# Attention followed by a gated FFN: how eighteen weight steps are spread, and how each finds its scale

## The chip, the cores and the metric

The kernel runs on one core of a Trainium2 chip. A core has five engines, each with an instruction queue of its own that it works off in order: TensorE (PE, matmuls; PEld is its weight load), VectorE (DVE), ScalarE (ACT), GpSimd (POOL) and SyncE (SP, which here only issues transfers). Sixteen DMA engines carry the transfers of all queues. The metric is the time of one execution in device microseconds (us).

## What is computed

```python
# attention: batch 8, heads 8, seq 576, head_dim 64, all float32
scores = q @ k.T / 8 + min(-(cum_i - cum_j), 0)   # cum: running sum of max(s, 0); causal mask
attn   = softmax(scores)
x      = (attn @ v), heads side by side           # 4608 tokens x 512
# gated FFN, weights float64: w_gate, w_val 512 x 1536; w_out 1536 x 512
out = (sigmoid(x @ w_gate) * (x @ w_val)) @ w_out # float32
```

## The kernel before

Attention goes head by head: 64 heads, numbered i, two of a pair sharing q, k and v tiles. A head has five query tiles of up to 128 rows. The main loop runs over *ticks* n; a tick is one query tile, so five ticks make one head. The first eight heads (batch 0, ticks 0 to 39) are computed with float32 matmuls; the later ones with q, k, probabilities and v split into float16 high and low parts, whose tiles are turned round by transposing transfers ("T<-qk", "pt<-p").

The result of a head pair is transposed on PE into a PSUM tile `nx_ps` and split into float16 parts x (L686, L688 on ACT, L689 on DVE). That PSUM tile has the tag "av" with one buffer.

The FFN works in units: a group of 256 tokens and one of 12 slices of 128 columns (`ffn_in`). A unit is 24 matmuls into a PSUM tile "gv" of two buffers (L714), a tanh on ACT (L719) and a product on DVE, `t2f` (L721). Groups 0 and 1 need only batch 0; their 24 units start at tick NE = 44 and fill PE's room beside the attention of the next heads. The second half of a unit (`ffn_out`, L744) needs all weights.

The weights arrive as float64 and are read as pairs of 32-bit integers. Eighteen *weight steps*, numbered n, turn them into float16 high and low parts: steps 0 to 11 one column slice of w_gate and w_val each (o = 0), steps 12 to 17 two row slices of w_out each (o = 1). A step is:

- two transfers of 512 KB (`load_weight`). Buffers rotate by three for steps 0 to 11: step n can be loaded and decoded when step n-3 has given back its buffers. Each `weight_step` also issues the loads that have become possible.
- `decode_weight`: a copy on ACT (L298) and three integer operations on DVE (L299, L300, L301) that rebuild a float32 in `a`. L299 leaves the magnitude's bits in `m`, which is the place where the result will go.
- a scale, a power of two. `split_weight` has two ways to find it. With `m`: `column_bound` sums the upper halves of `m` over the rows by eight matmuls with a matrix of ones into a PSUM tile `wps` (L310), takes the largest on DVE (L313), and two operations on one element a row make the scale (L332, L334). Without `m` (a path that the kernel has, and that float64 weights did not take): a Square on ACT with its sum along each row, a sum over the rows on POOL (`partition_all_reduce`), and `pow2_of`, two DVE operations.
- the high part, a copy with the scale on ACT (L337), and the low part on DVE (L338).

`column_bound` takes its PSUM tile from tag "av" (one buffer) up to tick 39 and from tag "o" (two buffers, shared with the outputs of attention and FFN) after it.

Steps 0 and 1 stand at tick 0 in the program, steps 2 to 5 at ticks 8, 16, 24 and 32; steps 6 to 17 are written between ticks 46 and 48, where the FFN's units call for them. The program order is not the order on the chip: a planner sorts the instructions of each engine by priority (program order, unless `first()` raises it) and by times that it works out itself, so that an instruction whose inputs and buffers are ready can come long before its place. `first()` is put around the float32 attention and, from tick 44 to 86, around the scores and outputs of the later heads.

Of the kernel before, what the change touches and what calls it, by code (L numbers as in the profile page):

```python
# [10 lines left out]
F32 = mybir.dt.float32  # L11
F32R = mybir.dt.float32r
I32 = mybir.dt.int32
I64 = mybir.dt.int64
AF = mybir.ActivationFunctionType
ALU = mybir.AluOpType
ADD_REDUCE = bass.bass_isa.ReduceOp.add

P = 128
# [6 lines left out]
def tile_attention_then_gated_ffn(  # L26
# [11 lines left out]
    nc = tc.nc  # L38
# [11 lines left out]
    NTL = len(TILES)  # L50
# [4 lines left out]
    NN = H  # L55
# [7 lines left out]
    pp = ctx.enter_context(tc.tile_pool(name="pp", bufs=2, space=bass.MemoryType.PSUM))  # L63
# [69 lines left out]
    wscale = cp.tile([P, 2, NF], F32, name="wscale")  # L133
# [8 lines left out]
    def first(now=True):  # L142
        return tc.high_priority(1000) if now else ExitStack()
# [80 lines left out]

    wide = w_gate.dtype == I64
    wst, wdec, wtot = {}, {}, {}

    rows_out = cp.tile([P, 2 * DM], F32, name="io")
    t2big = cp.tile([P, 2 * NF * GT], F32, name="t2f")
# [60 lines left out]
    def decode_weight(n):  # L290

        o, f = wsteps[n]
        r, a, _ = room(n)
        if not wide:
            return a.bitcast(F32), None
        m = w2all[:, f // 2].rearrange("p l h x n -> p (l h x n)") if o else w1[f].rearrange("p c g l n -> p (c g l n)")
        m = m.bitcast(I32)
        nc.scalar.activation(a.bitcast(F32), r[:, :, 1].bitcast(F32), AF.Copy, scale=2.0 ** -112)  # L298
        nc.vector.tensor_scalar(m, a, 3, 0x7FFFFFF8, ALU.logical_shift_left, ALU.bitwise_and)  # L299
        nc.vector.scalar_tensor_tensor(a, a, -0x80000000, m, ALU.bitwise_and, ALU.bitwise_or)  # L300
        nc.vector.scalar_tensor_tensor(a, r[:, :, 0], 29, a, ALU.logical_shift_right, ALU.bitwise_or)  # L301
        return a.bitcast(F32), m

    def column_bound(n, m):

        top = m.bitcast(BF16).rearrange("p (n t) -> p n t", t=2)[:, :, 1]
        early = wnext["tick"] < NTL * NN
        ps = pp.tile([P, 512], F32, tag="av" if early else "o", name=f"wps{n}", **({"bufs": 1} if early else {}))
        for c in range(8):
            nc.tensor.matmul(ps[:, :P], ones, top[:, c * P : (c + 1) * P], start=c == 0, stop=c == 7)  # L310
        tot = wp.tile([P, 1], F32, tag="wst", name=f"wtot{n}")
        junk = lp.tile([P, P], BF16, tag="wj", name=f"wj{n}")
        nc.vector.tensor_scalar(junk, ps[:, :P], 2.0 ** -100, None, ALU.max, ALU.max, accum_out=tot)  # L313
        return tot

    def split_weight(n, a, m):

        o, f = wsteps[n]
        if o:
            hi, lo = (w2all[:, f // 2, l].rearrange("p h x n -> p (h x n)") for l in range(2))  # L320
        else:
            a = a.rearrange("p (c n) -> p c n", n=P)
            hi, lo = (w1[f].rearrange("p c g l n -> p (c g) l n")[:, :, l] for l in range(2))
        if m is None:
            ss = wp.tile([P, 1], F32, tag="wss", name=f"wss{n}")
            nc.scalar.activation(hi, a, AF.Square, accum_out=ss)
            tot = wp.tile([P, 1], F32, tag="wst", name=f"wtot{n}")
            nc.gpsimd.partition_all_reduce(tot, ss, P, ADD_REDUCE)
            pow2_of(wscale[:, o, f : f + 1 + o], tot, f"w{n}")
        else:  # L330
            e = wp.tile([P, 1], I32, tag="xe", name=f"xe_w{n}")
            nc.vector.tensor_scalar(e, column_bound(n, m).bitcast(I32), 0x7F800000, None, ALU.bitwise_and)  # L332
            dst = wscale[:, o, f : f + 1 + o]
            nc.vector.tensor_scalar(dst.bitcast(I32), e.to_broadcast([P, 2]) if o else e, -1.0, 268.0 * 2.0 ** 23,  # L334
                                    ALU.mult, ALU.add)
        sc = wscale[:, o, f : f + 1]
        nc.scalar.activation(hi, a, AF.Copy, scale=sc)  # L337
        nc.vector.scalar_tensor_tensor(lo, a, sc, hi, ALU.mult, ALU.subtract)  # L338
# [21 lines left out]
        osc[b] = wp.tile([P, 1], F32, tag="osc", name=f"osc{b}", bufs=3)  # L360
        nc.vector.tensor_scalar(osc[b], gmax, sv[b][1], 2.0 ** 14, ALU.mult, ALU.mult)

    wnext = {"load": 0, "step": 0, "tick": 0}

    def weight_step():
        n = wnext["step"]
# [425 lines left out]
    NE, NOFF = 44, 87  # L792
# [6 lines left out]
    for n in range(nticks + 12):  # L799
        if n == NTL * EARLY:  # L800
            more_room()
        i, t = divmod(n, NTL)
        wnext["tick"] = n
        if i < NN:
            with first():
                n_s(i, NTL - 1 - t)
# [37 lines left out]
        if i < NH:  # L844
            p, j = divmod(i, 2)
            b, h = divmod(i, H)
            if t == 0 and i + 1 < NH:
                load_crow(i + 1)
            if t == (2 if i >= NN else 0) and i + 1 < NH:
                spread_crow(i + 1)  # L850
            if i + 2 < NN:
                if j == 0 and t == 1:
                    n_load(p + 1)
                    load_v(p + 1)
                if j == 1 and t == 2:
                    with first():
                        n_prep(p + 1)
            elif j == 0 and i + 2 < NH:
                if t == (2 if spare else 1 if i >= NN else 0) and p + 1 not in qk32:
                    load_qk(p + 1)  # L860
                if t == 2 and i < NN:
                    load_v(p + 1)
            if NN <= i and i + 1 < NH and j == 1 and t == 2:
                load_v(p + 1)
            if NN <= i and j == 0 and t == 0:
                split_v(p)
            if not spare:
                late = i >= NN
                if i + 2 >= NN and j == 0:
                    if t == 2 + late:  # L870
                        qk_square(p + 1)
                    if t == 3 + late:
                        qk_scale(p + 1)
                if n == NTL * (NN - 1) - 1 or NN <= i and t == 0:
                    split_qk(max(i + 1, NN))
                if n == NTL * (NN - 1) + 1 or NN <= i and t == 2:
                    swap_k(i + 1)
            elif i <= EARLY + 1:
                if j == 0:
                    if t == 1:  # L880
                        split_qk(i + 1)
                    if t == 3:
                        swap_k(i + 1)
                        load_qk(p + 2)
                else:
                    if t == 0:
                        qk_square(p + 1)
                    if t == 1:
                        qk_scale(p + 1)
                    if t == 2:  # L890
                        split_qk(i + 1)
                    if t == 4:
                        swap_k(i + 1)
                        split_qk(i + 2)
                        load_qk(p + 3)
            elif j == 0 and i + 2 < NH:
                if t == 0:
                    if i == EARLY + 2:
                        swap_k(i + 1)
                    qk_square(p + 1)  # L900
                if t == 1:
                    qk_scale(p + 1)
                if t == 2:
                    split_qk(i + 2)
                if t == 4:
                    swap_k(i + 2)
            elif j == 1 and i + 2 < NH:
                if t == 1:
                    split_qk(i + 2)
                if t == 3:  # L910
                    swap_k(i + 2)
                    if i + 6 < NH:
                        load_qk(p + 3)
            if b == 0:
                if 1 <= n < 1 + vch:
                    v_square(0, n - 1)
                if n == 1 + vch:
                    v_scale(0)
            if b == 0:
                if t == 2 and 1 <= h < 1 + vch:  # L920
                    v_square(1, h - 1)
                if t == 4 and 1 <= h < 1 + vch:
                    v_square_sum(1, h - 1)
                if t == 1 and h == 6:
                    v_scale(1)
            elif b == 1:
                if VSQ <= n < VSQ + vch:
                    v_square(2, n - VSQ)
                if VSQ + 5 <= n < VSQ + 5 + vch:
                    c = VSQ + 4 + vch - n  # L930
                    v_square_sum(2, c)
                if n == VSQ + 11:
                    v_scale(2)
            elif b + 1 < B:
                if t == 0 and 2 <= h < 2 + vch:
                    v_square(b + 1, h - 2)
                if t == 4 and 2 <= h < 2 + vch:
                    v_square_sum(b + 1, h - 2)
                if t == 4 and h == 2 + vch:
                    v_scale(b + 1)  # L940
            if n in OUT:
                load_weight(NF + OUT.index(n))
            while n < NE and wnext["step"] < min(2 + n // 8, 6):
                weight_step()

        if n >= NE and state["u"] < 2 * NF:
# [63 lines left out]
```

## Time and profile before

| what | value |
|---|---|
| median of 3 runs | 1151.53 us (1150.67 to 1153.77) |
| the profiled execution | 1150.28 us |
| its span, first to last instruction | 1148.5 us |
| PE busy | 1096.8 us (96%) |
| DVE busy | 756.4 us (66%) |
| ACT busy | 733.5 us (64%) |
| POOL busy | 199.9 us (17%) |
| granted TensorE clock, mean | 0.993 |
| column sums (L310) | 144 matmuls, 13.0 to 193.9 us |
| weight steps, first to last DVE operation (L299 to L338) | 11.7 to 208.4 us |

In lines of the profile, the engine and the source line stand first, then the operation, what it writes and reads (buffer numbers left out), shapes and count; "<-" behind a bar or in brackets names what the engine had been waiting for. A busy PE counts matmuls whose ends are modelled. Idle time of an engine matters only where another one waits for it.

### The profile page before, as it was taken

Reading aid. Unit: us, or ns where it says so; the run is one execution under the profiler, and the core shown is the slowest. Engines: PE = TensorE matmul, PEld = TensorE weight load, DVE = VectorE, ACT = ScalarE, POOL = GpSimd, SP = SyncE. Lnnn points to the kernel's source line nnn. Section 1 sums busy time; section 2 is a strip of 40 time slices with the busy share of each in tenths; the row PEclk is TensorE's granted clock in tenths of the full one; section 3 lists DMA queues with packets and bytes.
Section 4 is the critical chain, followed back from the end, with each engine's and each line's share of the span. In section 5 each row is a group of like instructions: output and inputs, shape, how many; then the busy total and the mean of one; then the engine's idle time right before and its main releaser. Section 6 shows DMA issues by size and latency. Waiting matters only on the chain.

```text
span 1148.5 us, 30266 instructions
## 1 busy us (share of the span) xinstructions
PE 1096.8 (96%) x11868; PEld 861.6 (75%) x11868; DVE 756.4 (66%) x2212; ACT 733.5 (64%) x1437; POOL 199.9 (17%) x473
## 2 busy tenths in 40 slices
PE   6998878999999999999999999999999999999998
PEld 4776757757777887788777777778877787787775
DVE  6868989876787777665565667777777775222222
ACT  5869667867776777676665667778676765233222
POOL 3301101022232222121211122212221211000000
PEclk9999999999999999999999999999999999999999
DMA  9766986997989688866645488878787774000000
GB/s 282 218 189 140 181 178 144 174 200 154 178 159 187 150 186 158 154 139 135 148 87 130 90 175 163 170 144 175 152 159 146 142 123 88 13 20 20 1 19 19
DMA packets 445517, 157.63 MB, mean 137 GB/s; under 512 B 403583, under 2 KB 435839, under 8 KB 445374
## 3 DMA queue, kind: packets, MB, share of 16 engines
q1 hardware_dynamic: 418686, 127.38, 56.7%
q10 hardware_dynamic: 23328, 17.04, 4.9%
q0 software_dynamic: 3360, 11.27, 2.8%
q8 instruction: 93, 1.52, 0.6%
q14 instruction: 50, 0.41, 0.1%
HBM read 56.92 MB, written 9.58 MB: 58 GB/s over the span
## 4 chain that ended last, share of the span: by engine, by line
PE 72%; DMA 10%; DVE 6%; issue 5%; ACT 3%; SPq 3%; POOL 1%; ACTq 0%; DVEq 0%; POOLq 0%
PE gv L714 39%; PE o L744 21%; DMA v<-in_v_dram 3%; PE s L491 3%; PE s L489 2%; DMA T<-qk 2%; PE na_ps L662 1%; SPq L463 1%; DVE e L529 1%; PE av L564 1%; PE av L562 1%; PE av L563 1%; DMA qk<-in_q_dram 1%; DMA w2all<-in_moe_w_out_dram 1%; PE s L631 1%
## 5 line engine op out<-in xcount | busy, mean ns | idle before, releaser
L714 PE MATMUL gv<-x,w 128*128 128x256 f16 (+3 forms) x6912 | 619.2, 247 | 10.1 <-DVE t2f L721 9.1
L714 PEld LDWEIGHTS <-w 128*128 128x128 f16 x6912 | 536.0, 98 | 75.0 <-issue 11.5
L744 PE MATMUL o<-w2all,h 128*128 128x512 f16 x1296 | 313.7, 379 | 1.8 <-ACT h L729 1.8
L530 ACT ACTIVATE e<-e,em 128x576 f32<-128x576 f32 x280 | 153.2, 556 | 92.5 <-DVE em L529 89.8
L744 PEld LDWEIGHTS <-h 128*128 128x128 f16 x1296 | 123.3, 98 | 109.1 <-ACT h L729 2.1
L719 ACT ACTIVATE th<-gv,scb 128x256 f32<-128x256 f32 (+3 forms) x288 | 110.8, 410 | 138.6 <-PE gv L714 130.5
L721 DVE SCALAR_TENSOR_TENSOR t<-th,gv 128x256 f32<-128x256 f32 x192 | 80.0, 417 | 147.9 <-ACT th L719 146.8
L511 POOL TENSOR_SCALAR_AFFINE_SELECT rl<-rl 128x128 f32<-128x128 f32 (+1 forms) x240 | 85.8, 358 | 503.1 <-DVE em L529 462.3
L529 DVE CUSTOM_DVE_ANT_0 e<-s,rl,qkcf 128x576 f32<-128x576 f32 x280 | 151.5, 545 | 31.7 <-PE s L491 15.6
L729 ACT ACTIVATE h<-t,hsc 128x256 f16<-128x256 f32 x192 | 96.7, 504 | 92.4 <-DVE t L721 92.4
L539 DVE SCALAR_TENSOR_TENSOR p<-e,p 128x384 f16<-128x384 f32 x224 | 103.1, 500 | 45.1 <-ACT p L534 44.3
L730 DVE SCALAR_TENSOR_TENSOR h<-t,hsc,h 128x256 f16<-128x256 f32 x192 | 93.7, 488 | 44.9 <-ACT h L729 42.6
L534 ACT ACTIVATE p<-e 128x1152 f16<-128x1152 f32 x112 | 111.9, 1000 | 2.7
L489 PE MATMUL s<-T 128*128 128x288 f16 (+2 forms) x246 | 64.1, 278 | 7.8 <-DVE em L529 4.0
L562 PE MATMUL av<-v,pt 128*128 128x65 f16 x560 | 67.7, 193 | 2.2 <-DMA pt<-p 2.2
L451 POOL PARTITION_BROADCAST cr<-cr x63 | 59.4, 947 | 56.0 <-DMA cr<-cum_d 42.0
L563 PE MATMUL av<-v,pt 128*128 128x64 f16 x560 | 67.7, 192 | 0.0
L564 PE MATMUL av<-v,pt 128*128 128x65 f16 x560 | 67.6, 194 | 0.0
L491 PE MATMUL s<-T 128*128 128x288 f16 (+2 forms) x246 | 61.5, 277 | 4.0 <-DMA T<-T 3.9
L562 PEld LDWEIGHTS <-pt 128*128 128x128 f16 x560 | 52.5, 97 | 7.9 <-DMA pt<-p 3.1
L563 PEld LDWEIGHTS <-pt 128*128 128x128 f16 x560 | 52.5, 97 | 4.5
L564 PEld LDWEIGHTS <-pt 128*128 128x128 f16 x560 | 52.7, 97 | 0.2
(164 smaller groups left out, 1297.0 us busy)
## 6 DMA issues: line engine op xcount, KB each, us to landing
v<-v SPq DMA_DIRECT2D x56, 162.5 KB
out_dram<-io POOLq DMA_DIRECT2D x34, 256.0 KB, 3.2
v<-in_v_dram SPq DMA_DIRECT2D x64, 128.0 KB
T<-T SPq DMA_DIRECT2D x82, 72.0 KB
t2f<-in_v_dram SPq DMA_DIRECT2D x20, 288.0 KB
qk<-in_q_dram SPq DMA_DIRECT2D x17, 288.0 KB
qk<-in_k_dram SPq DMA_DIRECT2D x17, 288.0 KB
w2all<-in_moe_w_gate_dram ACTq DMA_DIRECT2D x7, 512.0 KB
```

The lines of the kernel that those rows point to most:

```text
L491: nc.tensor.matmul(ps[:, : b_ - a], lhs, T[i][:, 2, a:b_], start=False, stop=not mask)
L529: nc.vector.tensor_tensor_reduce(e, ps, r, c, MASKED, ALU.add, ALU.min, acc)
L530: nc.scalar.activation(e_t[t][:, :w], e_t[t][:, :w], AF.Exp, bias=acc, scale=-1.0)
L534: nc.scalar.activation(p_s[h_][:, 0], e_s[h_], AF.Copy, scale=PSCALE)
L539: nc.vector.scalar_tensor_tensor(flat[:, LOW[t] * P : (LOW[t] + t) * P], e_t[t][:, : t * P], PSCALE, flat[:, kb * P : (kb + t) * P], ALU.m ...
L562: nc.tensor.matmul(AV[i][:, t], hi, v_[:, D : 2 * D + 1], start=kb == 0, stop=False)
L563: nc.tensor.matmul(AV[i][:, t, 0:D], hi, v_[:, 0:D], start=False, stop=False)
L564: nc.tensor.matmul(AV[i][:, t], lo, v_[:, D : 2 * D + 1], start=False, stop=False)
L714: nc.tensor.matmul(ps[:, gv, a:e], w1[f][:, cc, gv, wl], x_of(b, cc)[:, xl, c0 + a : c0 + e], start=(c == 0), stop=(c == 3 * NC - 1))
L719: nc.scalar.activation(th[:, a:e], ps[:, 0, a:e], AF.Tanh, scale=scb[b][:, f : f + 1])
L729: nc.scalar.activation(h[:, 0], t2, AF.Copy, scale=hsc[:, f : f + 1])
L744: nc.tensor.matmul(ps[:m], h[:, hl, tt * P : tt * P + m], w2[f][:, wl], start=(f == 0 and c == 0), stop=(f == NF - 1 and c == 2))
```

## The change

Three things change. The steps up to tick 43 are now one every five ticks, up to nine (`NSUM`): steps 0 and 1 at tick 0, then step 2 at tick 5, step 3 at tick 10 and so on to step 8 at tick 35. These nine have column sums, always in tag "av", and the sums and the two operations that make the scale are under `first()`. The other nine, steps 9 to 17, return no `m` and so take the path with a Square on ACT and POOL's sum. `wnext["tick"]` goes, as nothing else reads it.

```diff
+    NSUM = 9
...
-        return a.bitcast(F32), m
+        return a.bitcast(F32), m if n < NSUM else None
...
-        early = wnext["tick"] < NTL * NN
-        ps = pp.tile([P, 512], F32, tag="av" if early else "o", name=f"wps{n}", **({"bufs": 1} if early else {}))
+        ps = pp.tile([P, 512], F32, tag="av", name=f"wps{n}", bufs=1)
...
-            nc.vector.tensor_scalar(e, column_bound(n, m).bitcast(I32), 0x7F800000, None, ALU.bitwise_and)
-            dst = wscale[:, o, f : f + 1 + o]
-            nc.vector.tensor_scalar(dst.bitcast(I32), e.to_broadcast([P, 2]) if o else e, -1.0, 268.0 * 2.0 ** 23,
-                                    ALU.mult, ALU.add)
+            with first():
+                nc.vector.tensor_scalar(e, column_bound(n, m).bitcast(I32), 0x7F800000, None, ALU.bitwise_and)
+                dst = wscale[:, o, f : f + 1 + o]
+                nc.vector.tensor_scalar(dst.bitcast(I32), e.to_broadcast([P, 2]) if o else e, -1.0, 268.0 * 2.0 ** 23,
+                                        ALU.mult, ALU.add)
...
-    wnext = {"load": 0, "step": 0, "tick": 0}
+    wnext = {"load": 0, "step": 0}
...
-        wnext["tick"] = n
...
-            while n < NE and wnext["step"] < min(2 + n // 8, 6):
+            while n < NE and wnext["step"] < min(2 + n // NTL, NSUM):
                 weight_step()
```

## The prediction

> **What bounds the kernel now.** I read the page first (totals, then the slices), then the busy time of each engine by stretches of the span, then, for the one stretch that stands out, what TensorE waited for.
>
> ```profile
> PE 1096.8 (96%) x11868; PEld 861.6 (75%) x11868; DVE 756.4 (66%) x2212; ACT 733.5 (64%) x1437; POOL 199.9 (17%) x473
> PE   6998878999999999999999999999999999999998
> DVE  6868989876787777665565667777777775222222
> ```
>
> Over the whole span TensorE (PE) is the full engine, but the slices are not alike: PE dips in slices 3 to 6 (86 to 201 us), and just there VectorE (DVE) stands at 8 or 9. The next view puts numbers to it; its columns are the stretch, its length, the busy time of PE, PEld, DVE, ACT and POOL, the granted clock and the DMA share.
>
> ```profile
> 20.00:100.00 80.00, 70.97 (x534) 59.55 (x532) 56.19 (x164) 63.90 (x134) 16.77 (x28) 0.96 0.74 208
> 100.00:208.00 108.00, 86.96 (x961) 73.50 (x960) 100.96 (x276) 78.04 (x125) 11.79 (x16) 0.95 0.82 165
> 208.00:300.00 92.00, 85.24 (x954) 60.39 (x952) 66.17 (x202) 67.13 (x142) 18.01 (x40) 1.00 0.86 174
> 300.00:1148.00 848.00, 841.00 (x9360) 659.40 (x9358) 519.49 (x1538) 513.88 (x1019) 144.62 (x358) 1.00 0.59 120
> ```
>
> From 300 us on PE is idle 7 us in 848: what is won before is kept, as nothing later waits for a fixed time. From 100 to 208 us PE is idle 108 - 86.96 = 21.0 us, and DVE is busy 100.96 of 108 (93%): DVE bounds this stretch. From 20 to 100 us DVE has 23.8 us free. PE's waits from 100 to 220 us (total, times, longest):
>
> ```profile
> PE gv L714 <- DVE t2f L721: 9.1, 6, 3.3
> PE nx_ps L686 <- DVE x L689: 3.4, 1, 3.4
> PE s L489 <- DMA T<-qk: 3.3, 2, 2.4
> PE s L491 <- DMA T<-T: 2.8, 3, 1.9
> ```
>
> 12.5 us of the idle time wait for a DVE result, 6.1 us for transfers.
>
> **What a weight step costs** (groups of instructions up to 220 us: count | busy, mean ns):
>
> ```profile
> L299 DVE TENSOR_SCALAR w<-w2all 128x1024 int32<-128x1024 int32 x8 | 5.7, 709 | 2.2 <-ACT w2all L298 2.0
> L300 DVE SCALAR_TENSOR_TENSOR w2all<-w2all,w 128x1024 int32<-128x1024 int32 x8 | 9.7, 1212 | 0.1
> L301 DVE SCALAR_TENSOR_TENSOR w2all<-w2all 128x1024 int32<-128x1024 int32 x8 | 10.1, 1267 | 0.0
> L313 DVE TENSOR_SCALAR_CACHE_REDUCE wj<-wps 128x128 bf16<-128x128 f32 x18 | 5.0, 279 | 1.8 <-PE wps L310 1.8
> L313 DVE DVE_READ_ACCUMULATOR wj<-wps 128x1 f32 x18 | 1.4, 80 | 0.0
> L332 DVE TENSOR_SCALAR xe_w<-wtot 128x1 int32<-128x1 int32 x18 | 2.5, 142 | 0.0
> L334 DVE TENSOR_SCALAR wscale<-xe_w 128x1 int32<-128x1 int32 (+1 forms) x18 | 2.7, 148 | 0.0
> L338 DVE SCALAR_TENSOR_TENSOR w<-w2all,wscale,w 128x1024 f16<-128x1024 f32 x8 | 10.2, 1276 | 3.2 <-ACT w L337 3.2
> L298 ACT ACTIVATE w2all<-w2all 128x1024 f32<-128x1024 f32 x8 | 9.2, 1148 | 2.1 <-DMA w2all<-in_moe_w_val_dram 2.1
> L337 ACT ACTIVATE w<-w2all,wscale 128x1024 f16<-128x1024 f32 x8 | 9.1, 1141 | 0.1
> ```
>
> On DVE: decoding 0.71 + 1.21 + 1.27 = 3.19 us, the bound 0.28 + 0.08 = 0.36, the scale 0.29, the low part 1.28: 5.1 us a step, 92 us for 18. That is what fills DVE.
>
> **Edit 1: steps every five ticks, nine before tick 44.** The place in the program is not when a step runs. On DVE:
>
> ```profile
> 31.08 1.09 DVE L299 TENSOR_SCALAR w<-wa 128x1024 int32<-128x1024 int32 x1
> 54.27 0.44 DVE L689 SCALAR_TENSOR_TENSOR x<-nx_ps,vsc,x 128x256 f16<-128x256 f32 x1
> 57.84 1.28 DVE L338 SCALAR_TENSOR_TENSOR w<-wa,wscale,w 128x1024 f16<-128x1024 f32 x1 [1.35 <-ACT w L337]
> 61.59 0.69 DVE L299 TENSOR_SCALAR w<-wa 128x1024 int32<-128x1024 int32 x1
> 73.64 0.47 DVE L689 SCALAR_TENSOR_TENSOR x<-nx_ps,vsc,x 128x256 f16<-128x256 f32 x1
> 95.03 0.47 DVE L689 SCALAR_TENSOR_TENSOR x<-nx_ps,vsc,x 128x256 f16<-128x256 f32 x1
> ```
>
> and on PE:
>
> ```profile
> 54.91 0.62 PE L310 MATMUL wps<-w,ones 128*128 128x128 bf16 x8
> 74.42 0.62 PE L310 MATMUL wps<-w,ones 128*128 128x128 bf16 x8
> 95.56 0.64 PE L310 MATMUL wps<-w,ones 128*128 128x128 bf16 x8
> ```
>
> The buffers named "wa" serve steps 0, 3, 6 and 9. Step 3 is decoded from 31.1 us on, but its column sum runs at 54.9, directly behind the x of a head pair; those of steps 4 and 5 at 74.4 and 95.6, directly behind the next two. The sums share one PSUM buffer ("av") with the x and stand behind it in the program. And step 6 can be decoded (61.6) only when step 3 has given back its buffer (57.8). So the sums gate the whole pipeline: at 100 us eight steps are decoded but only five scaled.
>
> With a step every five ticks, steps 2 and 3 stand ahead of the first pair's x, 4 and 5 ahead of the second's, 6 and 7 ahead of the third's, 8 ahead of the fourth's. Each gains about one pair, some 20 us: steps 5, 6 and 7 are scaled before 100 us, step 8 near it. Moved out of the full stretch: four low parts 5.1, bounds of 6 to 8 1.1, scales 1.2, the decoding of step 8 3.2: 10.6 us of DVE. If steps 9 and 10, whose squares need no PSUM, come early too, 2 x 3.2 more; I take one of them: 13.8 us, between 10.6 and 17.
>
> What it costs before 100 us: that DVE work fits the 23.8 us free, and four ACT copies (4.6 us) and a decoding copy or two fit ACT's 16.1. But these are operations of 1.2 us on in-order queues of attention, whose chain passes DVE and ACT at each tile. An attention operation caught behind one loses half, 0.6 us. With some 17 more on both engines, a quarter of them caught costs 2.5 us; all caught, 10; none, 0. I take 2.5, since both engines keep free time. Each step also issues a later step's two loads on ACT's queue, for example:
>
> ```profile
> 86.45 0.39 ACTq L286 DMA_DIRECT2D w2all<-in_moe_w_gate_dram  x1
> ```
>
> At 0.4 us an issue that is nothing beside exps of the same queue. The bytes go from a stretch with DMA share 0.82 to one with 0.74; SP's queue is passed by nothing. I cost it at 0; if q and k come late by it, by one such load at most, some us.
>
> **Edit 2: high priority for sums and scales.** Eight matmuls take 0.62 us with the tail of the last, 0.46 without, and wait only for L299. Placed so early that PE stands still for that operation each time, they would cost 9 x 0.7 = 6 us; I take 0, since the matmuls of attention and, from 100 us, of the FFN can be put ahead of them, and keep the 6 in the upper end.
>
> **Edit 3: nine steps without column sums.** Gone from PE: 9 x 0.46 = 4.1 us. Gone from DVE: 9 x 0.36 = 3.2 us. Added on ACT, by the nearest rows (the squares of q and k):
>
> ```profile
> L403 ACT ACTIVATE jq<-qk 96x768 f16<-96x768 f32 x10 | 8.4, 837 | 4.3 <-DMA qk<-in_q_dram 4.3
> L403 ACT ACTIVATION_READ_ACCUMULATOR jq<-qk 96x1 f32 x10 | 1.9, 188 | 0.0
> ```
>
> 0.84 us for 768 elements is 1.12 for 1024 (the copy of that size: 1.14), and 0.19: 9 x 1.31 = 11.8 us, of which moved copies give back 5.7. ACT goes from 78 to 84 of 108: near DVE's new load, so I charge 1 us of the gain. On POOL:
>
> ```profile
> 140.94 1.21 POOL L406 PARTITION_ALL_REDUCE qkt<-ssq  x1 [3.97 <-ACT jq L403]
> 175.86 0.12 POOL L471 MEMSET v<- 128x20 f16 x1 [33.71 <-PE av L564]
> 183.49 0.41 POOL L406 PARTITION_ALL_REDUCE qkt<-ssq  x1 [4.64 <-ACT jq L403]
> 176.44 1.68 DVE L301 SCALAR_TENSOR_TENSOR wa<-w2all,wa 128x1024 int32<-128x1024 int32 x1
> ```
>
> A sum takes 0.41 us, or 1.21 beside DVE's two-input operations; the last row shows L301 at 1.68 instead of 1.22 while a POOL broadcast ran. I charge 9 x 0.1 = 1 us, between 0 and 9 x 0.46 = 4. [...]
>
> **The sum.** DVE's load in the stretch falls from 101.0 by 13.8 + 3.2 to 84, from 93% to 78%. Of the 12.5 us of waits for DVE I take 65%, 8.1. Some of these waits also slow PE after them:
>
> ```profile
> 113.46 5.32 PE L714 MATMUL gv<-x,w 128*128 128x256 f16 x28
> 160.31 2.78 PE L714 MATMUL gv<-x,w 128*128 128x256 f16 x24 [3.28 <-DVE t2f L721]
> ```
>
> 28 matmuls behind the 3.4 us wait for x took 5.32 us, where 24 others took 2.78: 2.1 us too long, at a granted clock below 1. I take 1.4 of it. [...] Of the 4.1 us of column sums I take 2, since PE is not the bound there. So -8.1 - 1.4 - 2.0 + 2.5 + 1 + 1 = -7.0. The profiled execution took 1150.28 (span 1148.5 and 1.8 around it), 1.25 under the median of the runs: 1143.3 against it, 1144.5 against the median. At the ends: all terms full and no cost, 12.5 + 2.1 + 4.1 = 18.7 less, 1132.8; nothing won and the early cost of 2.5 to 10 paid, 1154 to 1161.
>
> **The rivals.**
>
> (a) *The room is filled by the next limit* (no change). DVE is relieved, but split q and k pass DVE, ACT and transposing transfers in turn, and PE's 6.1 us for transfers grow as the others shrink. For it: ACT at 84, and DMA share 0.82. Against it: the waits for DVE are the larger. Given back 5 of the 7.0: 1149.5.
>
> (b) *A sum stuck on POOL* (slower). POOL works in order and stood 33.71 us before the memset at 175.86, until PE had released a buffer of v. If a weight's sum lies behind such a memset, ACT's copy L337 waits for it, behind that the exps, behind DVE's low part attention and PE. Against it: the order is planned with times, and the same sum for q and k at 140.94 went ahead of that memset. One sum caught for half the wait, 17 us, of which ACT and DVE hide some 3: 1144.5 + 14 = 1158. It decides from about 7 us of standstill on.
>
> (c) *Nothing moves*, as steps 6 and 7 were decoded early anyway: PE's 4.1 of column sums and DVE's 3.2 alone, half of it on the path, and the early cost: 1150.5.
>
> **How the numbers follow.** Forecast 0.62, (a) 0.13, (b) 0.16, (c) 0.09. A difference of 0.3% (3.5 us) is about what a measurement of this kernel can tell from none. The forecast's cases lie below 1148, with its own range 1133 to 1148; (a) and (c) within 0.3%, 0.22 together with a little on each side; (b) above, 0.16. For 8 in 10 I leave out the far end of the gain and half of (b): 1134 to 1157. Faster 0.62, same 0.21, slower 0.17.
>
> **What the profile after would show.** Right: nine groups of eight column-sum matmuls, the ninth before about 100 us; steps 3, 4 and 5 scaled some 20 us sooner; DVE from 100 us below 85% and PE's waits for t2f under 4 us; no clock dip about 110 us; nine squares of about 1.1 us on ACT and nine sums of 0.4 to 1.2 on POOL. Wrong: PE's busy share from 20 to 100 us below 88%; ACT or DVE waiting for POOL's sum for several us; the waits for T grown by what t2f gave up.

## The result: 0.6% slower

The changed kernel takes 1159.39 us (median of 6 runs, 1156.75 to 1160.27) against 1152.17 us (6 runs, 1150.67 to 1155.94). The ratio is 1.0059, 95% interval 1.0039 to 1.0079. The forecast was 1144.5 us, and the measured time lies above the range of 1134 to 1157. The profiled execution took 1156.75 us, its span is 1155.0 (before: 1148.5). In the changed kernel every line of the source behind L226 stands one further down (L714 is now L715).

Totals and slices of the page after:

```profile
PE 1103.4 (96%) x11796; PEld 863.5 (75%) x11796; DVE 757.6 (66%) x2194; ACT 744.5 (64%) x1455; POOL 205.9 (18%) x482
PE   6898688899899999999999999999999999999998
DVE  6968999665687777766565577777777775222222
PEclk9997799999999999999999999999999999999999
```

PE has 72 matmuls fewer in its records and yet is busy 6.6 us longer; its idle time is 1155.0 - 1103.4 = 51.6 us, before 51.7. So the 6.5 us of span are all busy time of PE. The clock's row shows a 7 in slices 3 and 4 (87 to 144 us). By the same stretches as in the prediction:

```profile
20.00:100.00 80.00, 69.18 (x517) 56.28 (x516) 63.50 (x174) 66.42 (x131) 16.90 (x27) 0.97 0.78 226
100.00:208.00 108.00, 90.11 (x852) 72.87 (x853) 97.30 (x269) 88.96 (x157) 18.19 (x25) 0.86 0.83 160
208.00:300.00 92.00, 85.73 (x929) 61.78 (x927) 59.79 (x175) 62.04 (x128) 16.89 (x39) 0.98 0.78 153
```

From 100 to 208 us PE is busy 3.2 us *more* with 109 matmuls *less* (852 for 961; 84 of the 109 are column sums: 92 of their matmuls fell in this stretch before, 8 after), at a clock of 0.86 instead of 0.95. PE's waits from 100 to 220 us:

```profile
PE s L490 <- DVE em L530: 5.4, 4, 2.8
PE s L490 <- DMA T<-qk: 5.0, 3, 2.2
PE av L563 <- DMA pt<-p: 3.3, 6, 0.9
PE gv L715 <- DVE t2f L722: 2.4, 2, 2.0
```

Two of these waits were small before:

```profile
PE s L489 <- DVE em L529: 0.9, 1, 0.9
PE av L562 <- DMA pt<-p: 0.3, 1, 0.3
```

The wait for t2f fell from 9.1 to 2.4 us and that for x from 3.4 to 0.5. Those for em, for pt and for T<-qk (3.3 before) took their place.

**Where the clock went.** The trace gives the clock as 1.0 or 0.5. The stretches at 0.5, busy time and clock in each, before:

```profile
25.59:32.42 6.83, 6.27 (x28) 5.69 (x29) 4.02 (x12) 5.84 (x14) 1.96 (x3) 0.50 0.67 222
110.93:117.75 6.82, 4.74 (x23) 3.46 (x24) 6.82 (x21) 6.82 (x12) 0.00 (x0) 0.50 0.45 110
165.54:168.96 3.42, 3.42 (x16) 2.30 (x17) 2.63 (x6) 2.45 (x4) 0.00 (x0) 0.50 1.10 265
```

and after (the two longest, and the sum of all nine):

```profile
98.97:112.62 13.65, 11.44 (x58) 10.21 (x59) 11.42 (x28) 10.62 (x19) 5.13 (x5) 0.50 0.47 96
119.45:129.69 10.24, 6.26 (x30) 4.21 (x31) 10.24 (x27) 8.50 (x16) 1.49 (x4) 0.50 0.63 98
sum 45.67, PE 37.10 PEld 28.30 DVE 34.69 ACT 32.08 POOL 11.97; mean PE 4.12 PEld 3.14 DVE 3.85 ACT 3.56 POOL 1.33
```

This gives a ledger in three lines, which the experiments below use. *Clock loss* is half of PE's busy time in stretches at half clock (in 11.44 us there, 5.72 us of work were done): successive 256-column matmuls of L714 (after: L715) start 0.213 us apart there and 0.109 at full clock, in both traces. *Idle* is the span less PE's busy time. *Work* is the rest, the matmuls counted at full clock.

| us | idle | work | clock loss | span |
|---|---|---|---|---|
| before | 51.7 | 1089.6 | 7.2 | 1148.5 |
| after | 51.6 | 1084.9 | 18.6 | 1155.0 |
| difference | -0.1 | -4.7 | +11.4 | +6.5 |

That "work" is a real quantity is seen across kernels: in the seven profiles with eighteen column sums and no added matmuls it comes out at 1087.7 to 1090.0, in the five with nine sums at 1084.0 to 1085.0, while their spans differ by 11 us. Nor is the clock that of one odd execution: the mean granted clock was 0.977 to 0.983 in the six runs of the changed kernel, and 0.984 to 0.993 in all runs of the kernel before (means of a set 0.989 to 0.991). The profile of before has a high clock for that kernel, though, 0.993. By the mean clock of all runs, 0.990 and 0.980, some 23 us of a run stand at half clock before and 46 after (the profiles: 17.1 and 45.7). With PE as busy there as in the profiles (0.85 and 0.81) I estimate from this some 9 us of clock loss between the kernels instead of 11.4; of the 7.2 us between the medians, about 3 are then idle time.

PE's thin stretch lasts until head 8, the first with float16 scores, begins. Its first maximum on DVE, before (L529) and after (L530):

```profile
97.94 0.82 DVE L529 CUSTOM_DVE_ANT_0 e<-s,rl,qkcf 128x576 f32<-128x576 f32 x1 [0.71 <-PE s L518]
```

```profile
111.15 0.82 DVE L530 CUSTOM_DVE_ANT_0 e<-s,rl,qkcf 128x576 f32<-128x576 f32 x1 [2.23 <-PE s L519]
```

13.2 us later. In between PE has only the tail of the float32 heads to do.

### The profile page after: what moved, and what is told of

Its sections match the earlier page's. It is cut to its first block, busy times and chain, and to the rows that moved or that the text cites. A ratio compares the mean times of both kernels' runs of the same rounds, so it can differ in the third digit from the quotient of the medians.

```text
span 1155.0 us, 30145 instructions
## 1 busy us (share of the span) xinstructions
PE 1103.4 (96%) x11796; PEld 863.5 (75%) x11796; DVE 757.6 (66%) x2194; ACT 744.5 (64%) x1455; POOL 205.9 (18%) x482
## 4 chain that ended last, share of the span: by engine, by line
PE 72%; issue 8%; DMA 6%; DVE 6%; ACT 5%; POOL 2%; SPq 2%; ACTq 0%; POOLq 0%; DVEq 0%
PE gv L715 39%; PE o L745 21%; PE s L490 2%; PE s L492 2%; DMA v<-in_v_dram 2%; DVE e L530 1%; PE av L563 1%; PE av L565 1%; PE av L564 1%; POOL rl L512 1%; DMA pt<-p 1%; PE s L632 1%; PE na_ps L663 1%; SPq L464 1%; DMA qk<-in_k_dram 1%
## 5 line engine op out<-in xcount | busy, mean ns | idle before, releaser
L715 PE MATMUL gv<-x,w 128*128 128x256 f16 (+3 forms) x6912 | 619.1, 247 | 3.4 <-DVE t2f L722 2.4
L715 PEld LDWEIGHTS <-w 128*128 128x128 f16 x6912 | 536.1, 98 | 67.2 <-issue 4.6
L530 DVE CUSTOM_DVE_ANT_0 e<-s,rl,qkcf 128x576 f32<-128x576 f32 x280 | 151.4, 545 | 42.7 <-PE s L492 23.8
L490 PE MATMUL s<-T 128*128 128x288 f16 (+2 forms) x246 | 65.3, 283 | 11.3 <-DVE em L530 6.2
L563 PE MATMUL av<-v,pt 128*128 128x65 f16 x560 | 68.8, 193 | 4.0 <-DMA pt<-p 3.9
L492 PE MATMUL s<-T 128*128 128x288 f16 (+2 forms) x246 | 62.8, 281 | 4.1 <-DMA T<-T 4.0
L563 PEld LDWEIGHTS <-pt 128*128 128x128 f16 x560 | 52.8, 98 | 11.5 <-DMA pt<-p 6.1
```

The lines of the kernel that those rows point to most:

```text
L530: nc.vector.tensor_tensor_reduce(e, ps, r, c, MASKED, ALU.add, ALU.min, acc)
L563: nc.tensor.matmul(AV[i][:, t], hi, v_[:, D : 2 * D + 1], start=kb == 0, stop=False)
L715: nc.tensor.matmul(ps[:, gv, a:e], w1[f][:, cc, gv, wl], x_of(b, cc)[:, xl, c0 + a : c0 + e], start=(c == 0), stop=(c == 3 * NC - 1))
```

## The experiments

Theories at the start. *Crowding* (C): weight operations of the early steps stand in front of the preparation of q and k for head 8, on ACT and DVE, and delay it. *Late path* (L): the squares on ACT and the sums on POOL cost the time. *Priority* (P): the raised sums and scales do. *Gate* (G): whatever makes PE's use thin, the half clock that follows is what costs. Every kernel was timed in turns with the kernel before on the same chip.

**1. Each edit alone, on the kernel before.**

pace_alone:

```diff
-            while n < NE and wnext["step"] < min(2 + n // 8, 6):
+            while n < NE and wnext["step"] < min(2 + n // NTL, 9):
```

> The kernel before with edit 1 alone: a step every five ticks, nine before tick 44; all eighteen keep column sums at the old priority, in the old PSUM tags. Theory C (crowding): weight operations that the planner pulls into the run-up to head 8 delay its q and k on ACT and DVE. Then most of the loss is here: the first max of head 8 on DVE (128x576, 97.9 us before, 111.2 with the change) stands at 106 or later, and the kernel is 3 to 8 us slower than before. Theory L (the late path): the squares on ACT and POOL's sums, and the column sums missing on PE, cost the time after 100 us. Then this kernel is within 3 us of before or up to 5 faster, and head 8 starts by 101.

priority_alone:

```diff
-            nc.vector.tensor_scalar(e, column_bound(n, m)...
+            with first(n < 9):
+                nc.vector.tensor_scalar(e, column_bound(n, m)...
```

> The kernel before with edit 2 alone: column sums and scales of steps 0 to 8 at high priority, pace and way to the scale as before. Theory C: steps 3 to 5 still stand behind the x of a pair in the PSUM tag, so little moves: within 2 us of before, head 8 starts at 97 to 100. Theory P (the priority itself makes PE wait for decoding, or puts sums ahead of attention): slower by 3 us or more, with PE waits for L299 above 2 us.

squares_alone:

```diff
-        return a.bitcast(F32), m
+        return a.bitcast(F32), m if n < 9 else None
```

> The kernel before with edit 3 alone: steps 9 to 17 take the square on ACT and the sum on POOL; pace and priority as before. Theory C: head 8 starts near 98 to 101 as before, DVE is relieved by 3 us and PE by 4 from 100 us on, so the kernel is 0 to 5 us faster than before. Theory L: slower by 4 us or more, with the TensorE clock at half for longer than the 17 us (of the first 200) of before, or waits of ACT and DVE on POOL's sum of 5 us or more.

| kernel | median us | ratio, 95% interval | head 8, us | idle + work + clock loss (profiled run) |
|---|---|---|---|---|
| pace_alone | 1160.51 | 1.0084 (1.0057 to 1.0111) | 108.2 | 50.9 + 1090.0 + 10.2 = 1151.0 |
| priority_alone | 1161.07 | 1.0067 (1.0040 to 1.0095) | 100.8 | 58.1 + 1089.4 + 11.7 = 1159.2 |
| squares_alone | 1151.88 | 1.0003 (0.9987 to 1.0019) | 98.5 | 54.0 + 1084.9 + 11.5 = 1150.4 |

The squares and POOL's sums cost nothing by themselves, against L (beside the other two edits this is less clear, see part 3). Nor do they win anything: in the profiled runs the 4.7 us of work that they take off PE come back as 4.3 of clock loss and 2.3 of idle time. Pace and priority cost about as much as the whole change, each by itself. pace_alone ran at 1152.8 us in its profiled execution (clock 0.991) and at 1159.6 to 1162.9 in six others (0.976 to 0.981), with one program. A second profile of it:

pace_alone_again (the same kernel):

> The kernel of pace_alone once more, instruction for instruction. Its profiled execution took 1152.8 us at a mean granted clock of 0.991, six others 1159.6 to 1162.9 at 0.976 to 0.981. Theory G (the gate: the loss is TensorE running at half clock after low use, not the order of the work): an execution near 1160 agrees with the quick one, instruction by instruction, up to a stretch of half clock, and loses the 8 us in and behind it, with nearly the same PE idle time. Theory C (the order itself loses it: weight operations ahead of q and k): the same heads come late in both, by the same time, and the difference is spread over the whole span.

1155.94 us (one run), clock 0.984, head 8 at 112.8 us; 48.2 + 1089.6 + 16.4 = 1154.2. Against the first profile: work the same, idle 2.7 us less, clock loss 6.2 more.

Priority alone relieves t2f too, and hands the time to the transposed q and k, from 3.3 to 8.6 us (100 to 220 us):

```profile
PE s L490 <- DMA T<-qk: 8.6, 2, 4.7
PE s L492 <- DMA T<-T: 4.8, 2, 3.9
PE nx_ps L687 <- DVE x L690: 4.2, 1, 4.2
PE gv L715 <- DVE t2f L722: 3.1, 3, 1.2
```

**2. What delays head 8.** On the changed kernel, with first() also round the preparation of q and k (changed_qk_first), and with the copy that opens steps 9 to 17 kept in its place in the program (changed_late_held):

```diff
+                with first(n < NE):
+                    if i + 2 >= NN and j == 0: ...   # qk_square, qk_scale, split_qk, swap_k
```

> The changed kernel, and beside it the squares, scales, splits and swaps of q and k up to tick 43 (those of heads 8 and 9) at high priority, so that weight operations do not go ahead of them. Theory C: the chain from q and k to head 8 is free again, its first max comes at 98 to 104 instead of 111, the granted clock stays up between 100 and 130 us, and the kernel is 5 us or more faster than the changed one, at or below before. Theory L: head 8 comes earlier, but the time stays within 3 us of the changed kernel (1159.4).

```diff
+        if n >= NSUM:
+            tc.keep_in_program_order(ins)
```

> The changed kernel with the first copy on ACT of steps 9 to 17 pinned behind everything that stands before it on ACT in the program, so that these steps don't run ahead of tick 46. That takes two decodings, two squares and a low part out of the run-up to head 8. Theory C: head 8's first max comes at 105 us or earlier instead of 111, and the time falls by 4 us or more, to at most 1155. Theory G: head 8 comes a few us earlier at most, and the time goes with the granted clock: 1155 or less only if the mean clock is 0.987 or more.

The first came out with the same order of instructions on PE, DVE and ACT as the changed kernel, so it says nothing of priority; as a repeat it gave 1159.7 us, 1.0071 (1.0043 to 1.0098). The second: 1159.38 us, 1.0058 (1.0036 to 1.0080), head 8 still at 112.6. But what it held back is a step of w_out alone, whose copy came at 134.3 us instead of 83.4. The square of step 9 and the copy of step 10 still run ahead of head 8, as in the changed kernel:

```profile
91.72 1.06 ACT L328 ACTIVATE w<-wa 128x1024 f16<-128x1024 f32 x1 [0.40 <-DVE wa L304]
97.74 1.14 ACT L299 ACTIVATE w2all<-w2all 128x1024 f32<-128x1024 f32 x1
```

So it doesn't settle whether the steps behind 8 stand in the way. Where head 8's time goes can be read on ACT, which squares and splits its q and k. The second square and the split of q, before:

```profile
85.23 0.85 ACT L403 ACTIVATE jq<-qk 96x768 f16<-96x768 f32 x1
89.24 0.61 ACT L428 ACTIVATE qk<-qk,qksc 96x384 f16<-96x384 f32 x1
```

and after, with the weight operations about them:

```profile
90.27 1.06 ACT L326 ACTIVATE w<-wa 128x1024 f16<-128x1024 f32 x1 [0.41 <-DVE wa L302]
91.33 1.13 ACT L338 ACTIVATE w<-w2all,wscale 128x1024 f16<-128x1024 f32 x1
92.37 0.83 ACT L404 ACTIVATE jq<-qk 96x768 f16<-96x768 f32 x1
96.29 1.13 ACT L299 ACTIVATE w2all<-w2all 128x1024 f32<-128x1024 f32 x1
97.32 0.61 ACT L429 ACTIVATE qk<-qk,qksc 96x384 f16<-96x384 f32 x1
```

Against before, the load of q is issued 3 us later (78.60 for 75.65), the second square starts 7.1 us later, the split 8.1, the transposing transfer behind it 10.2 (101.27 for 91.05), and the first maximum 13.2. From 82 to 98 us ACT runs six weight operations of 1.06 to 1.15 us, of steps 6, 7, 9, 10 and w_out; before, none begins between 81 and 100 us. This is crowding, read in one trace of each kernel; no run takes these six away.

Then the early steps, on the kernel before: pace_cap6 has steps 2 to 5 at the new pace and 6 to 8 where they were; three_late is written as the reverse.

```diff
-min(2 + n // 8, 6)
+min(2 + n // NTL, 6)                           # pace_cap6
+min(2 + n // 8, 6) + max(0, (n - 33) // 3)     # three_late
```

> The kernel before with steps 2 to 5 at the new pace (one each five ticks instead of eight) and steps 6 to 8 left where they were, behind tick 44. Crowding just ahead of head 8 (steps 6 to 8 are what delays it): head 8's first maximum at 96 to 101 us as before, time 1151 to 1154 us. Rival, density from the start (any denser step pushes the heads behind it): head 8 at 103 us or later, time 1157 to 1161 us. Rival, order alone (any other order of the early weight work lets the clock fall): head 8 at 96 to 101 us and yet 1157 to 1161 us.

> The kernel before with steps 0 to 5 at the old pace and three more steps (6 to 8) at ticks 36, 39 and 42. Crowding just ahead of head 8: head 8 at 105 to 112 us, half-clock stretches of 30 us or more in all, time 1157 to 1162 us. Density from the start: head 8 below 103 us, time 1151 to 1155 us. Order alone: 1157 to 1161 us wherever head 8 comes.

pace_cap6: 1161.68 us, 1.0091 (1.0063 to 1.0120); three_late: 1161.64 us, 1.0086 (1.0064 to 1.0109). Head 8 in each:

```profile
109.12 0.82 DVE L529 CUSTOM_DVE_ANT_0 e<-s,rl,qkcf 128x576 f32<-128x576 f32 x1 [1.08 <-PE s L518]
```

```profile
98.92 0.82 DVE L529 CUSTOM_DVE_ANT_0 e<-s,rl,qkcf 128x576 f32<-128x576 f32 x1 [0.86 <-PE s L518]
```

My own form of C, that it takes steps 6 to 8 to crowd head 8, is wrong: the denser steps 2 to 5 alone delay it by 11 us. What steps 6 to 8 would do isn't shown, since three_late didn't bring them ahead of head 8 on the chip: their column sums run at 101.5, 104.2 and 107.7 us (before: 99.3, 105.9, 108.0). The planner made of it nearly the program of priority_alone: all 2212 operations of DVE stand in the same order, on PE all but 26 of 11868, on ACT all but two of 1437. It is a repeat of that kernel, at 1161.64 for 1161.07 us (ledger 53.8 + 1087.7 + 14.2 = 1155.7). Both say that a late head 8 is not needed for the loss: it begins at 98.9 and 100.8 us there.

**3. Two edits together.** changed_old_pace is the changed kernel with the old pace line; pace_and_priority the change without its squares.

> The changed kernel with the old pace (a step each eight ticks, six in all before tick 44): what is left of the change is the priority of the sums and the squares from step 9 on. If the pace is the cause of the loss: 1151 to 1154 us with head 8 below 102 us. If the priority costs as much by itself, as it did alone: 1158 to 1162 us with head 8 still near 100 us, and waits for the transposed q and k.

> The change without its squares: new pace and priority, column sums for all eighteen steps. If pace and priority each cost their own 8 to 9 us and add: 1167 to 1170 us. If both lead to the same thing (a late head 8 and a fallen clock once): 1158 to 1162 us, head 8 at 107 to 115 us, as the changed kernel. If the squares were what the changed kernel gained back, this one lies 3 us or more above it (1163 and up).

changed_old_pace: 1160.45 us, 1.0082 (1.0059 to 1.0104), head 8 at 99.0, ledger 60.0 + 1085.0 + 14.0, with 11.2 us of waits for T<-qk, as the second case had it. pace_and_priority: 1155.64 us, 1.0036 (1.0018 to 1.0053), head 8 at 109.8, ledger 50.5 + 1088.2 + 15.1. Two edits that cost 0.84% and 0.67% alone cost 0.36% together: nothing adds, and no edit has a price of its own. Nor did the third case come: without its squares the change is 4 us quicker, not slower (1.0036 against 1.0059 and, in the repeat, 1.0071). The intervals overlap, so a cost of the squares beside the other two edits is neither shown nor excluded. In all of these the work is as expected and the difference is clock loss, idle time, or both.

**4. The clock itself.** If G holds, more matmuls at the right place should make the kernel quicker. The fillers write 256 columns into a PSUM tile that the next matmul of the program overwrites. First in the score banks of heads 8 to 12, three in each (90 matmuls), on the changed kernel (changed_warm) and the kernel before (before_warm):

```diff
+        for ps in bank if i < WARM else ():          # WARM = 13
+            for _ in range(3):
+                nc.tensor.matmul(ps[:, :2 * P], w1[0][:, 0, 0, 0], ..., start=True, stop=True)
```

> The changed kernel with three matmuls of 256 columns before the scores of each bank of heads 8 to 12, into the same PSUM bank, which the scores then overwrite: 90 matmuls, 9.6 us of PE at full clock, that do nothing but keep PE at work while q and k are waited for. Theory G: the clock from 100 to 150 us goes from 0.74 to above 0.9 and the time falls by 3 us or more from 1159.4 in spite of the added work. Theory C: PE's waits are filled or not, head 8 stays at 111 us or later, and the time is the same or up to 10 us higher.

> The kernel before with the same 90 matmuls. It has only 6.8 us of half clock about 110 us and 3.4 about 167 to win back. Theory G: within 3 us of before, either way (up to 5 us of clock won, up to 9.6 us of work added, part of it in waits). Theory C: 3 to 10 us slower.

changed_warm: 1162.03 us, 1.0080 (1.0060 to 1.0101), ledger 49.1 + 1093.1 + 15.1: 8.2 us of work added, 3.5 of clock loss and 2.5 of idle time won. before_warm: 1154.17 us, 1.0022 (1.0003 to 1.0042), 46.4 + 1098.0 + 6.0. The fillers do act on the clock (mean of the runs 0.985 on the changed kernel, without them 0.980; 0.992 and 0.990 on the kernel before), but most come too late: nine run at 97.7 us, the next only at 114.1, behind a stretch at half clock from 103.3 to 113.6. So they were moved to where the clock falls: ahead of each of the five groups of transposes of head 7, eight in each (40 matmuls).

```diff
             ps = pp.tile([P, 512], F32, tag="gv", name=f"nt_ps_{i}_{t}_{a}")
+            for _ in range(8 if i == 7 else 0):
+                nc.tensor.matmul(ps[:, :2 * P], w1[0][:, 0, 0, 0], ..., start=True, stop=True)
```

> The changed kernel with eight filler matmuls of 256 columns ahead of each of head 7's five groups of transposes (40 matmuls, some 4.4 us of PE at full clock; what they write is overwritten). They lie at about 85 to 102 us. If thin use of PE starts the half clock: the stretch from 99.0 us (13.7 us) goes or shrinks to 7 us or less, clock loss 12 to 15 us instead of 18.6, PE's idle time 1 to 3 us less, time 1155 to 1159 us. If the half clock has another cause (the chain of the day, the heat of what ran before): the stretch stays, clock loss 18 to 21 us, time 1161 to 1164 us.

1153.29 us (12 runs), 1.0027 (1.0005 to 1.0050): six us *quicker* than the changed kernel, with 5.6 us more work. The fillers run from 97.2 to 109.7 us. Its profile:

```profile
97.16 1.04 PE L654 MATMUL nt_ps<-w 128*128 128x256 f16 x8
98.03 0.49 PE L657 MATMUL nt_ps<-ident,e 128*128 128x128 f32 x3
98.56 0.41 PE L690 MATMUL nx_ps<-ident,nx 128*128 128x128 f32 x2
100.39 0.44 PE L666 MATMUL na_ps<-v,p 128*128 128x65 f32 x2 [1.43 <-ACT p L658]
...
sum 24.65, PE 17.94 PEld 13.95 DVE 21.59 ACT 23.30 POOL 6.02; mean PE 3.59 PEld 2.79 DVE 4.32 ACT 4.66 POOL 1.20
```

The same 1.43 us wait for ACT stands there as in the changed kernel, but the half clock from 99 us is gone; the stretches at half clock hold 17.94 us of busy time instead of 37.10. Ledger 51.0 + 1090.5 + 9.0 = 1150.5. Head 8 is as late as in the changed kernel (first transposing transfer of its q and k issued at 101.7 us, there 101.3).

One profile says little of the stretch from 99 us, as the grid on which the clock changes lies elsewhere in each execution (last section): changed_qk_first, with the order of the changed kernel and a clock of 0.979, has none there either, but one from 55.1 to 68.8 us. All runs say more: the mean clock of the 12 is 0.986, against 0.980 in the changed kernel, some 13 us less at half clock. At the 0.41 us lost per us there (18.6 of 45.7) I estimate 5 us of clock won. Up to 100 us the instructions of DVE and ACT stand in the order of the changed kernel; from 102 us on the planner's order is another one, and what changes in idle time behind that can come from the order as well as from the fillers.

Half of the filler, four in each group:

> changed_warm_turns with four fillers in each of head 7's five groups instead of eight (20 matmuls, 2.2 us of work at full clock). If the amount of work at 97 to 110 us decides: the clock holds only in part, clock loss 11 to 16 us, time 1154 to 1158 us. If any use in the gap between 97 and 100 us is enough: clock loss 8 to 10 us as with eight, work 2 us lower, time 1150 to 1153 us.

> The same kernel as changed_warm_turns_half, for a profile of one of its quick runs. If their gain is the clock: in a run at 1150 us or less the clock loss is 6 to 11 us instead of 22.1, idle time 47 to 51 us, work 1085 to 1088 us, and no half-clock stretch of 10 us or more between 50 and 115 us. If the quick runs gain otherwise: clock loss 15 us or more, and idle time under 45 us. Median over the runs 1147 to 1153 us.

1149.29 us (12 runs), 0.9995 (0.9970 to 1.0021), and in a second set 1149.80 us (12 runs), 0.9992 (0.9975 to 1.0009). Twenty useless matmuls take 10 us off the changed kernel and bring it level with the kernel before; that it beats it isn't shown, as both intervals hold 1. One program ran from 1145.1 (clock 0.988) to 1159.1 us (0.978). The profiles of the two sets fell on both ends: 49.5 + 1085.8 + 22.1 = 1157.4 and 46.4 + 1087.3 + 12.7 = 1146.4. The order of instructions is the same in both, and 9.4 of the 11.0 us between them are clock loss, the rest idle time less work. The clock loss of the second, 12.7, is above the 6 to 11 expected; against the changed kernel it gains 5.9 by the clock and 5.2 by idle time.

Three fillings did not help. With the full filler in the first three groups only (`8 if i == 7 and t > 2 else 0`):

> changed_warm_turns with its eight fillers only in head 7's first three groups (24 matmuls, 2.6 us; they lie at about 97 to 103 us), the two behind them (106 to 110 us, ahead of head 8's scores) left out. If the gap at 97 to 100 us is what starts the half clock: no stretch from 99 us, clock loss 8 to 11 us, work 2 us lower, head 8's scores up to 2 us sooner, time 1149 to 1153 us. If the fillers at 106 to 110 us held the clock: a stretch of 7 us or more between 103 and 118 us, clock loss 13 to 18 us, time 1156 to 1160 us.

1157.63 us, 1.0048 (1.0022 to 1.0075), ledger 53.4 + 1089.0 + 12.6. No stretch begins at 99 us here either, as the first theory has it, but the time is that of the second, and the clock loss lies between the two: idle time is 2.4 us above that of the five places, and half clock stands for 32.4 us in all, there 24.6. Over all runs the mean clock is 0.986 with three places and with five, so the 4 us between their medians are not clock. Which of the two last places matters, and why, isn't settled. And two in each score bank of heads 8 and 9 (24 matmuls), on the kernel before and on squares_alone:

> The kernel before with two filler matmuls of 256 columns in each score bank of heads 8 and 9 (24 matmuls, 2.2 us of work). If a little work is enough to hold the clock: the stretch from 110.9 us (6.8 us) goes, clock loss 5 to 6 us instead of 7.2, idle time 1 to 3 us less, time 1149 to 1152 us. If only a dense filling holds it (the 90 fillers of before_warm): clock loss 7 to 11 us, time 1153 to 1156 us.

> squares_alone with the same 24 fillers. squares_alone had 54.0 us of idle time, 1084.9 of work and 11.5 of clock loss. If the nine column sums that the squares take off PE had kept its clock up, and fillers do the same: clock loss 6 to 8 us, work 1087, time 1147 to 1150 us, under both kernels. If the fillers do nothing for the clock: 1153 to 1156 us.

1155.94 us, 1.0039 (1.0023 to 1.0054), 53.0 + 1091.9 + 9.0; and 1160.61 us, 1.0077 (1.0053 to 1.0101), 62.3 + 1088.2 + 12.0. In front of scores that others wait for, these 24 keep no clock (clock loss 9.0 for 7.2 and 12.0 for 11.5), and idle time is 1.3 and 8.3 us above that of the kernels without them; the 90 of before_warm did keep some (6.0 for 7.2). So what fillers were worth differed here with the place and with the number.

## Why the prediction was wrong, step by step

- **Waits for DVE, -8.1 us: right for the two waits that I read, worth nothing in sum.** t2f fell by 6.7 us and x by 2.9, and DVE's last low part of a weight came 19 us sooner (188.1 for 207.1). But PE's idle time as a whole moved by -0.1 in the profiles. DVE's load from 100 to 208 us went from 101.0 to 97.3, where I had 84: from 20 to 100 us it rose by 7.3, of 13.8 forecast, and other work moved up, as from 208 to 300 us it fell by 6.4. Rival (a), to which I gave 0.13 and 5 us of give-back, is nearest: the room was filled by em (0.9 to 5.4), which is a DVE result too, and pt (0.3 to 3.3). The waits for T that (a) named did not grow in sum (6.1 to 5.9).
- **The slow clock, -1.4 us: the step that failed.** I counted one stretch at half clock that would go with its wait, and never asked whether the change would make others. It is +11.4 by the ledger, some 9 by the clocks of all runs. The 3.4 us wait for x in that stretch (110.9 to 117.8) did go, and stretches of 13.65 and 10.24 us stand there instead. My reading that PE ran slowly only behind this wait was wrong too:

```profile
107.51:110.93 3.42, 1.74 (x19) 1.16 (x18) 3.42 (x13) 3.03 (x6) 0.50 (x1) 1.00 0.74 127
113.01 0.66 PE L686 MATMUL nx_ps<-ident,nx 128*128 128x128 f32 x2 [3.40 <-DVE x L689]
```

The wait runs from 109.6 to 113.0 us, so the half clock began 1.3 us into it, at 110.9, behind a window in which PE was busy for half of the time (1.74 of 3.42 us).

- **Column sums off PE, -2.0:** mis-sized; the ledger has the full 4.7 (I had 4.1 and took half).
- **Early cost, +2.5:** in the stretch where I placed it, about right: PE is busy 1.8 us less from 20 to 100 us. Mis-sized in what follows: I priced the operations that get caught, not head 8, which comes 13.2 us late and leaves PE thinly used until then. A load's issue, put at 0 by one row of 0.4 us, can cost more: one took 2.61 us, 8 us ahead of head 8's first square, and ACT stood still for 2.25 of them.

```profile
78.91 2.61 ACTq L287 DMA_DIRECT2D w2all<-in_moe_w_gate_dram  x1
81.56 0.40 ACT L622 COPY nk<-nq_ps 128x288 f32<-128x288 f32 x1 [2.25 <-issue]
```

- **Edit 2, taken at 0: not borne out.** Alone it makes the kernel 0.67% slower. The price that I named, PE standing still for L299, is absent: 0.5 us in all, as before. What grew is the wait for T<-qk (3.3 to 8.6 us).
- **ACT +1 and POOL +1:** both absent in squares_alone, which is at 1.0003; beside the other edits not settled (part 3). The squares take what was forecast (below), and the sums 0.38 us in the median, 2.19 at most. Rival (b) did not occur: POOL waited for the squares, and nobody for POOL's sums but one operation of its own and, once for 0.7 us, DVE.

```profile
L326 ACT ACTIVATE w2all<-io 128x1024 f16<-128x1024 f32 x3 | 3.2, 1052 | 0.7 <-DVE io L302 0.7
L326 ACT ACTIVATION_READ_ACCUMULATOR w2all<-io 128x1 f32 x3 | 0.6, 186 | 0.0
```

Of the list of things to be seen: nine groups of sums, t2f under 4 us and the squares came as said, and so did POOL's sums but for the one of 2.19 us; the ninth sum came at 102.8 instead of before about 100; steps 3 to 5 were scaled 12 to 33 us sooner; DVE from 100 to 208 us stands at 90%, not below 85%; the clock dip about 110 us is there, and longer. The sign "PE's busy share from 20 to 100 us below 88%" did show, at 86%.

What stays open: why priority alone makes the transposed q and k late, why pace and priority together lose less than each, and which of the weight operations ahead of head 8 make it late. The ledger says in which currency each loses, not which instruction began it. That thin use of PE goes ahead of half clock is shown by the windows below (72 of 72 at a share under 0.4), and that fillers on the changed kernel raise the clock by the runs (means of 0.985 and 0.986 for 0.980); that the clock alone is the loss of every variant is not (changed_old_pace and priority_alone lose 6 to 8 us of idle time), and about half of what the fillers win is idle time (5.2 against 5.9 us in the profile of half_fillers_again).

## What to carry to other kernels

On a kernel whose main engine is nearly full, split the span into idle time, work and clock loss before forecasting: a stall or an early start is worth what it does to all three, and a shorter wait says nothing by itself (here the wait for t2f fell by 6.7 us, idle time by 0.1). A change that moves side work forward should be read for the stretch that it leaves thin, in windows of a few us; here twenty matmuls put there took 10 us off, where the removed column sums were 4.7 us of work. One profile of such a kernel is one draw (one program ran from 1145.1 to 1159.1 us), so the clock of all runs belongs beside it.

## What the hardware showed

In all twenty profiles every stretch at half clock begins on one grid of 3.413 us, exact to 0.001 of a step, and lasts a whole number of steps (but for the one that reaches the span's end); the grid's place against the start of the span differs from execution to execution (1.70 us before, 3.40 after). All twenty, cut on their own grids from the first record of the clock (at 10 to 14 us) to 400 us, by PE's busy share in a window at full clock:

| busy share of the window | windows | followed by half clock |
|---|---|---|
| under 0.4 | 72 | 72 |
| 0.4 to 0.5 | 56 | 31 |
| 0.5 to 0.6 | 66 | 12 |
| 0.6 to 0.7 | 100 | 4 |
| 0.7 and more | 1780 | 0 |

Of 43 windows at half clock with a share under 0.7, none was followed by full clock, of 147 above it 119 were. The two windows of the changed kernel ahead of its longest stretches:

```profile
95.57:98.99 3.42, 2.08 (x16) 1.45 (x15) 2.76 (x8) 3.42 (x8) 0.78 (x1) 1.00 0.12 28
116.05:119.47 3.42, 1.21 (x9) 0.67 (x8) 3.42 (x11) 3.42 (x7) 0.16 (x1) 1.00 0.38 86
```

The second, at 0.35, is as the table has it; the first, at 0.61, is one of the four exceptions in its row (the ends of matmuls are modelled, and the rows from 0.4 to 0.7 hold both outcomes). PE was idle through neither of them: it was busy for 2.08 and 1.21 us of 3.42, and the longest single waits that begin there are 1.43 and 1.24 us. What the table shows is a share: half clock followed all 72 windows in which PE was busy for under 40% of the time, and 31 of the 56 between 40 and 50%. The grid's place differs from execution to execution, so a stretch near that share can fall either way: the one from 99.0 us is at half clock in the profile of the changed kernel and not in that of changed_qk_first, with the same order of instructions. This fits the spread of one program between 1145.1 and 1159.1 us at clocks of 0.988 and 0.978; that it is the cause of all of it was only argued.
